# Top-32 attention feeding a two-layer MLP on one core: a hand-written drain, early copies on another engine, first attention products one slot later

## The chip, the cores and the metric

The kernel runs as one program on one core of a Trainium2 chip. The core has a matrix engine (TensorE, PE in the profile), a vector engine (VectorE, DVE), an activation engine (ScalarE, ACT), a general engine (GpSimd, POOL) and a queue processor that issues most transfers (SyncE, SP). Each engine takes its own instructions strictly in the order of its stream and waits on semaphores for the others. The metric is the device time of one execution in microseconds; the smaller the better. Times are medians of several executions.

## The reference, cut to what matters

```python
B, H, S, D = 8, 8, 576, 64
scores = q @ k.T / sqrt(D)                       # per batch and head, 576 x 576
kth    = 32nd largest of each row
attn   = softmax(where(scores >= kth, scores, -1e9))
x      = (attn @ v) -> [4608 tokens, 512]        # heads side by side
h      = x @ w_in                                # 512 x 2048
g      = max(h, 0) + alpha * min(h, 0)
out    = g @ w_out                               # 2048 x 512
```

So each of 64 x 576 rows of 576 scores needs its 32nd largest value, and everything below it is dropped before the softmax. The MLP follows on the tokens of a batch.

## The kernel before, in words

**Units.** A *duo* is two row blocks of 128 query rows by 576 scores: the same block j of the two heads of one pair p ("n" duos), or the last 64 rows of two pairs ("m" duos, the tails). The list `duos` (lines 77 to 83) has 18 duos for each of the 8 batches, 144 in all (ND). In a batch the order is blocks 0 and 1 of the four pairs, two tails, then blocks 2 and 3 of the four pairs; in the last batch the blocks go one after the other, block 0, tails, block 1, 2, 3.

**One slot per duo.** The main loop (line 722) runs slots n = 0 to ND + 3. Each engine's stream is written out by hand, since the wrapper `Ordered` (line 21) keeps program order; that wrapper issues every instruction, so every row of the profile names its line 32. A duo d goes through stages, each some slots later than the one before:

- slot d - 1: `st_qk` (233), scores in PSUM by TensorE; then `st_exit` (255), ScalarE copies them to SBUF (`s_sb`).
- slot d: `dve_slot` (313), VectorE takes the 8 largest of each of 6 groups of 96 columns (`up`, `small`) and, for each pair of duos, a lower bound of the 32nd largest (`p`, in `threshold_steps`, 285).
- slot d + 2: `st_count` (395), ScalarE counts by Sign which scores lie above the bound (`sg`); `st_y` (407), GpSimd multiplies the scores by the signs (`y`); then `row` (282), VectorE takes the 8 next candidates (`p` <- `y`).
- slot of the even partner + 4: the three `pick_steps` (265), VectorE picks the 32nd largest into KT, scaled by 2^60.
- slot d + 4: `st_relu` (414), ScalarE makes a bf16 tile that is huge wherever the score is below the 32nd largest (`r`), and GpSimd subtracts it from the scores in place (`s_sb` <- `s_sb`, `r`).
- slot d + 5: `st_exp` (422), ScalarE takes Exp of the masked scores into one of three tiles `w`, and SyncE issues the transpose of `w` into one of three tiles `wT`.
- slot d + 7: `st_av` (429), TensorE multiplies `wT` with v and a column of ones (an *AV*, 10 matmuls) into the single PSUM tile `xo`; at the odd duo of a pair `norm_a` and `norm_b` (454, 459) divide on VectorE, and `st_xT` (482) has the result of a whole block transposed by SyncE.

**The MLP beside it.** When a block's transposed tile is complete, `mlp_ready` (510) queues its work: *hidden units* `ph` (16 matmuls for 128 tokens, 512 values per partition), each followed by one Relu to `gT` on VectorE (`h_dve`, 566), and *output parts* `pz` (5 matmuls, four parts to 128 tokens), each four followed by one ScalarE copy `o_sb` (`o_act`, 577) and a store. The hidden units have two PSUM buffers, which the transposes of q and k and the filler matmuls (`rest`, `keep_warm`, 560) share; the output has one PSUM tile, so that parts wait for the copy. Blocks are taken as chunks of 256 tokens, in the last batch of 128 tokens. `h_pe` (547) and `o_pe` (572) place a unit or a part in a slot when there is one; otherwise the filler is placed.

**The start.** In slots 0 to 3 the transposed q and k (`tps`) are copied from PSUM to `qkT`; the copies of 512 columns (two each in slots 0 and 2) are on VectorE (line 773). The weights of the MLP are loaded and scaled in slots 2 to 15.

**The end.** Duos of the last four (140 to 143) have their own lags in `stage` (381 to 393); the four slots after 143 have the AVs first, and a loop (784) works off what is left of the MLP. Masking there goes as before: Relu on ScalarE, subtraction on GpSimd, Exp on ScalarE.

Of the kernel before, what the change touches and what calls it, by code (L numbers as in the profile page):

```python
# [8 lines left out]
FP32 = mybir.dt.float32  # L9
# [8 lines left out]
NG = 6  # L18
# [41 lines left out]
def fast_path(tc, q, k, v, moe_w_in, moe_w_out, moe_alpha, out, flag):  # L60
# [17 lines left out]
    for b in range(B):  # L78
        p0 = KPB * b
        last = b == B - 1  # L80
        half = lambda j, n: [("n", p, j + i) for p in range(p0, p0 + KPB) for i in range(n)]
        tails = [("m", p0, p0 + 1), ("m", p0 + 2, p0 + 3)]
        duos += half(0, 1) + tails + half(1, 1) + half(2, 1) + half(3, 1) if last else half(0, 2) + tails + half(2, 2)
# [4 lines left out]
    with ExitStack() as ctx:  # L88
# [171 lines left out]
        def norm_of(n):  # L260

            m = n - 7 if n < ND + 1 else {ND + 1: ND - 5, ND + 2: ND - 3, ND + 3: ND - 1}.get(n, 0)
            return m if m > 0 and m % 2 else 0
# [49 lines left out]
        def dve_slot(n, f_late):  # L313

            norm = norm_of(n)
            rows = [d for d in duos_at("row", n)]
            picks = [f for m in duos_at("pick", n) for f in pick_steps(m)]
            if on(n):
                s = T["s", n]
                if n % 2 == 0:  # L320
                    T["up", n // 2] = two.tile([128, 4, NG // 2, 8], FP32, name="up", tag="up")
                up = T["up", n // 2]
                for i in range(2):
                    r = 2 * (n % 2) + i
                    for g in range(NG):
                        o = 24 * r + 8 * (g // 2)
                        m = DVE.max(out=(lo if g % 2 else up)[:, r, g // 2, :],
                                    in_=s[:, i, GW * g:GW * g + GW])
                        if g % 2:
                            sm(m, [], [(o, o + 8)])  # L330
                            if picks:
                                picks.pop(0)()
                if n % 2 == 0:
                    h_dve()
                    for d in rows:
                        row(d, 0)
                    if norm:
                        norm_a(norm)
                    for d in rows:
                        row(d, 1)  # L340
                    if norm:
                        norm_b(norm)
                else:
                    fold, negate, least, turn = threshold_steps(n // 2)
                    fold()
                    h_dve()
                    negate()
                    for d in rows:
                        row(d, 0)
                    least()  # L350
                    turn()
                    for d in rows:
                        row(d, 1)
            else:
                if norm:
                    norm_a(norm)
                    norm_b(norm)
                early = picks and duos_at("pick", n)[0] < ND // 2 - 1
                if early:
                    for f in picks:  # L360
                        f()
                if not norm:
                    h_dve()
                for d in rows:
                    row(d, 0)
                    row(d, 1)
                if not early:
                    for f in picks:
                        f()
                if norm:  # L370
                    h_dve()
            if f_late:
                h_pe()
                h_dve()
# [6 lines left out]
        for d in range(ND):  # L381
            last = d - (ND - 4) if d >= ND - 4 else None
            for kind, lag, drain in (("count", 2, (2, 2, 2, 1)), ("relu", 4, (4, 3, 3, 2)),
                                     ("exp", 5, (5, 4, 4, 3)), ("av", 7, (6, 5, 5, 4))):
                at_slot = d + (lag if last is None else drain[last])
                if d < ND - 4:
                    at_slot = min(at_slot, ND + 1)
                stage.setdefault((kind, at_slot), []).append(d)
        for (kind, n), l in list(stage.items()):
            if kind == "count":  # L390
                stage["row", n] = l
        for m in range(ND // 2):
            stage["pick", 2 * m + (4 if m < ND // 2 - 1 else 3)] = [m]

        def st_count(n):
            s, p9 = T["s", n], T["p9", n // 2]
            sg = two.tile([128, 2, S], BF16, name="sg", tag="sg", bufs=3)
            if n % 2 == 0:
                T["cs", n // 2] = three.tile([128, 4], FP32, name="cs", tag="cs")
            cs = T["cs", n // 2]  # L400
            for i in range(2):
# [3 lines left out]
            T["sg", n] = sg  # L405
# [16 lines left out]
        def st_exp(n):  # L422
            w = ws[n % 3]
            ACT.activation(w[:, :, 0:S], T.pop(("s", n)), AF.Exp, scale=att_scale)
            wt = three.tile([128, 10, 128], BF16, name="wT", tag="wT")
# [3 lines left out]
        def st_av(n):  # L429
            d = duos[n]  # L430
            wt = T.pop(("wt", n))
            if n % 2 == 0:
                T["xo", n // 2] = ps_x.tile([128, 2, 2, 65], FP32, name="xo", tag="x")
# [48 lines left out]
        def st_xT(n):  # L482
            d = duos[n]
            b = d[1] // KPB
            if d[0] == "n":
# [3 lines left out]
                one = b == B - 1  # L489
# [18 lines left out]
        soon, hq, oq, act, stores, late_o = [], [], [], [], [], [0]  # L508
# [569 lines left out]
```

## Time and profile before

| | us |
|---|---|
| median of 3 executions | 839.28 (837.2 to 839.58) |
| the profiled execution's own time | 840.79 |
| its span, first to last instruction | 839.0 |

The profiled execution is 1.51 us above the median; 1.79 us of its own time lie outside its span. The page gives the busy time of each engine, the span in 40 slices, the chain of work that ended last, and groups of instructions with their mean duration and the idle time ahead of them. A row of the timeline reads: start, duration, engine, operation, output <- inputs, shapes, count, and in brackets the idle time before it with what ended it. Durations overlap by the pipeline's length, so what one more instruction costs in a row of equal ones is read from start to start.

### The profile page before, as it was taken

The page shows a single profiled execution, that of the slowest core. Times are in us where ns is not written, and L with a number is a line of the kernel's source. Part 1 is how long each engine was busy: PE and PEld are TensorE (multiplying, and loading weights), DVE is VectorE, ACT ScalarE, POOL GpSimd, SP SyncE. Part 2 cuts the span into 40 slices and gives each one's busy share as a digit, 9 for nine tenths or more (in the row PEclk, how much of TensorE's full clock was granted, in tenths as well). Part 3 has the DMA queues.
Part 4 walks back from the last instruction along what each step waited for, and adds up shares of the span by engine and source line. Part 5 has one row for each costly group of instructions (what it writes and reads, how often), then busy time and mean ns, then how long its engine had stood idle before and what let it go on. Part 6 is the DMA issues. An engine that isn't in the chain of part 4 may idle for free.

```text
span 839.0 us, 17803 instructions
## 1 busy us (share of the span) xinstructions
PE 751.4 (90%) x5382; PEld 426.0 (51%) x5382; DVE 759.2 (90%) x3475; ACT 763.5 (91%) x1255; POOL 753.7 (90%) x706
## 2 busy tenths in 40 slices
PE   8878798998989898898989899898989899989696
PEld 5334344555545554455545455555545555456463
DVE  4879977999999999999999999999999999999731
ACT  4789988999999999999999999999999999999820
POOL 1798988999999999999999999999999999999920
PEclk9979899999999999999999999999999999999898
DMA  6599867556656556556656556556666555444441
GB/s 142 157 165 182 157 124 151 92 122 134 118 120 131 109 103 148 107 133 120 128 114 142 112 96 143 107 132 121 131 113 142 120 96 103 88 83 79 81 87 41
DMA packets 344231, 100.19 MB, mean 119 GB/s; under 512 B 338032, under 2 KB 338048, under 8 KB 344128
## 3 DMA queue, kind: packets, MB, share of 16 engines
q1 hardware_dynamic: 341152, 92.13, 55.6%
q0 software_dynamic: 1776, 6.56, 3.2%
q8 instruction: 44, 0.72, 0.3%
q14 instruction: 59, 0.48, 0.2%
q10 hardware_dynamic: 1200, 0.30, 0.2%
HBM read 36.71 MB, written 9.44 MB: 55 GB/s over the span
## 4 chain that ended last, share of the span: by engine, by line
DVE 38%; POOL 19%; ACT 17%; PE 15%; issue 6%; DMA 3%; SPq 0%; ACTq 0%; POOLq 0%
DVE small L32 11%; DVE p L32 10%; POOL y L32 9%; POOL s_sb L32 9%; DVE up L32 7%; DVE gT L32 5%; ACT r L32 5%; ACT sg L32 5%; PE ps_sc L32 4%; ACT s_sb L32 4%; PE pz L32 3%; ACT w L32 3%; PE ph L32 3%; PE rest L32 2%; DMA wT<-w 2%
## 5 line engine op out<-in xcount | busy, mean ns | idle before, releaser
L32 POOL TENSOR_TENSOR y<-s_sb,sg 128x576 f32<-128x576 f32 x288 | 362.1, 1278 | 40.6 <-ACT sg L32 40.0
L32 POOL TENSOR_TENSOR s_sb<-s_sb,r 128x576 f32<-128x576 f32 x288 | 362.3, 1279 | 8.9 <-ACT r L32 8.6
L32 ACT ACTIVATE sg<-s_sb,p 128x576 bf16<-128x576 f32 x288 | 221.4, 773 | 8.0 <-DVE p L32 6.8
L32 DVE MAX8 p<-y 128x8 f32<-128x576 f32 x288 | 215.1, 747 | 8.1 <-POOL y L32 7.6
L32 DVE MAX8 up<-s_sb 128x8 f32<-128x96 f32 x864 | 211.8, 245 | 9.8 <-ACT s_sb L32 9.8
L32 DVE MAX8 small<-s_sb 128x8 f32<-128x96 f32 x864 | 216.1, 250 | 0.0
L32 ACT ACTIVATE r<-s_sb,KZ 128x576 bf16<-128x576 f32 x288 | 206.6, 769 | 0.4 <-DVE KZ L32 0.4
L32 PE MATMUL ps_sc<-qkT 64*128 64x512 f32 (+2 forms) x768 | 184.1, 569 | 18.7 <-ACT s_sb L32 18.6
L32 ACT COPY s_sb<-ps_sc 128x1152 f32<-128x1152 f32 x144 | 159.2, 1105 | 21.8 <-PE ps_sc L32 21.5
L32 ACT ACTIVATE w<-s_sb 128x1152 bf16<-128x1152 f32 x144 | 166.4, 1156 | 5.9 <-POOL s_sb L32 5.8
L32 PE MATMUL ph<-xT,w_in_b 128*128 128x256 bf16 (+1 forms) x1408 | 150.8, 255 | 5.3 <-ACT qkT L32 2.9
L32 PE MATMUL pz<-w_out_b,gT 128*128 128x512 bf16 x576 | 148.8, 381 | 0.3 <-DVE gT L32 0.3
L32 PEld LDWEIGHTS <-w_in_b 128*128 128x128 bf16 x1408 | 119.2, 99 | 48.7 <-issue 12.0
L32 PE MATMUL xo<-v,wT 128*128 128x65 bf16 (+3 forms) x1600 | 127.0, 199 | 11.2 <-DMA wT<-w 11.2
L32 PEld LDWEIGHTS <-wT 128*128 128x128 bf16 (+3 forms) x1600 | 97.9, 100 | 40.3 <-DMA wT<-w 11.8
L32 DVE TENSOR_SCALAR gT<-ph 128x512 bf16<-128x512 f32 x144 | 97.2, 675 | 19.4 <-PE ph L32 19.3
L32 PEld LDWEIGHTS <-gT 128*128 128x128 bf16 x576 | 55.9, 98 | 71.9 <-issue 16.9
L32 PEld LDWEIGHTS ps_sc<-qkT 64*128 64x128 f32 (+1 forms) x768 | 56.0, 170 | 64.4 <-ACT s_sb L32 30.3
L32 PEld LDWEIGHTS ps_sc<-kd,qkT 128*128 128x128 f32 x256 | 38.3, 189 | 97.7 <-issue 95.4
L32 PE MATMUL pz<-w_lin_b,xT 128*128 128x512 bf16 x144 | 55.6, 386 | 16.4 <-ACT o_sb L32 16.3
L32 PE MATMUL rest<-idle 128*128 128x512 bf16 x224 | 62.4, 409 | 8.6 <-DVE gT L32 5.2
L32 PE MATMUL ps_sc<-kd,qkT 128*128 128x128 f32 x256 | 62.8, 327 | 0.0
(57 smaller groups left out, 572.2 us busy)
## 6 DMA issues: line engine op xcount, KB each, us to landing
k_st<-in_k_dram SPq DMA_DIRECT2D x64, 128.0 KB, 2.8
v_st<-in_v_dram SPq DMA_DIRECT2D x64, 128.0 KB, 2.7
q_st<-in_q_dram SPq DMA_DIRECT2D x62, 128.0 KB, 2.8
out_dram<-o_sb SPq DMA_DIRECT2D x31, 256.0 KB, 2.5
w_st<-in_moe_w_out_dram POOLq DMA_DIRECT2D x4, 1024.0 KB, 6.6
wT<-w SPq DMA_TRANSPOSE x144, 3.5
w_in_b<-in_moe_w_in_dram POOLq DMA_DIRECT2D x4, 512.0 KB, 6.5
k_st<-in_k_dram SPq DMA_DIRECT2D x32, 32.0 KB, 2.7
```

Of the source, the lines that this page charges most:

```text
L32: ins = self.tc.keep_in_program_order(f(*a, **kw))
```

## The change

Four things are edited.

1. **The copies of the start.** The 512-column copies of `tps` to `qkT` in slots up to 3 are ScalarE's (`n > 3 and ...` in the condition).
2. **The first AVs.** For duos 0 to 12 the AV, and for the odd ones among them the normalization, come in slot d + 8 in place of d + 7; duos 12 and 13 fall together in slot 20.
3. **The next to last batch.** It ends with block 2 of the four pairs and then block 3, as two chunks of 128 tokens, in place of both blocks of each pair as one chunk of 256; the loads and transposes of pair 30 come two slots later.
4. **The drain.** The loop ends at slot 143. Behind it stands a list written out by hand. For duos 140 to 143 Relu and subtraction are gone: `st_all` takes Exp of the raw scores into an fp32 tile `e_sb`, and `st_mask` multiplies it on VectorE by (score >= 32nd largest), one instruction per row block, into `w`. The PSUM tile of the scores, free by then, becomes `spare`: its first bank is a second output tile, its two others hold the AVs of duos 140 to 143. Relus of hidden units go to VectorE and ScalarE by turns.

```diff
+        elif b == B - 2:
+            duos += half(0, 2) + tails + half(2, 1) + half(3, 1)
...
-            for kind, lag, drain in (("count", 2, (2, 2, 2, 1)), ("relu", 4, (4, 3, 3, 2)),
-                                     ("exp", 5, (5, 4, 4, 3)), ("av", 7, (6, 5, 5, 4))):
...
+            for kind, lag in (("count", 2), ("relu", 4), ("exp", 5), ("av", 8 if d < 13 else 7)):
+                stage.setdefault((kind, d + lag), []).append(d)
...
+            stage["norm", d + (8 if d < 13 else 7)] = d
...
-                one = b == B - 1
+                one = b == B - 1 or b == B - 2 and j > 1
...
-                on_dve = short and n > 16 or wide and (n < 17 or n % 2 == 0)
+                on_dve = n > 3 and (short and n > 16 or wide and (n < 17 or n % 2 == 0))
...
+        def picked(m):
+            for f in pick_steps(m):
+                f()
+            kv = T["kv", m] = two.tile([128, 4], FP32, name="kv", tag="kv")
+            DVE.tensor_scalar(kv, KT[:, 4 * m:4 * m + 4], 1.0 / BIG, None, ALU.mult)
+
+        def st_all(d):
+            e = T["e", d] = qk_p.tile([128, 2, S], FP32, name="e_sb", tag="qkT")
+            ACT.activation(e, T["s", d], AF.Exp, scale=att_scale)
+
+        def st_mask(d):
+            w, e, s_ = ws[d % 3], T.pop(("e", d)), T.pop(("s", d))
+            kv = T["kv", d // 2]
+            for i in range(2):
+                r = 2 * (d % 2) + i
+                DVE.scalar_tensor_tensor(out=w[:, i, 0:S], in0=s_[:, i, :], scalar=kv[:, r:r + 1],
+                                         in1=e[:, i, :], op0=ALU.is_ge, op1=ALU.mult)
+            st_wT(d)
...
+        def fill(k):
+            for _ in range(k):
+                if not o_pe() and not h_pe(2):
+                    keep_warm()
+
+        D = ND - 1
+        now[0] = ND
+        T["spare"] = ps_s.tile([128, 1536], FP32, name="spare", tag="s")
+        o_sp()
+        st_av(D - 6)
+        h_pe(2)
+        h_pe(2)
+        st_count(D - 1)
+        st_y(D - 1)
+        picked(D // 2 - 1)
+        h_relu()
+        normed(D - 6)
+        h_relu()
+        o_act()
+        st_all(D - 3)
+        st_all(D - 2)
+        fill(1)
+        h_pe(2)
+        st_av(D - 5)
+        st_mask(D - 3)
+        st_mask(D - 2)
+        st_count(D, (0,))
+        h_relu(ACT)
+        st_count(D, (1,))
+        st_y(D)
+        fill(1)
+        h_pe(2)
+        st_exp(D - 4)
+        h_relu(ACT)
+        o_act()
+        now[0] += 1
+        for d in (D - 1, D):
+            row(d, 0)
+            row(d, 1)
+        st_all(D - 1)
+        st_all(D)
+        picked(D // 2)
+        st_mask(D - 1)
+        st_mask(D)
+        o_sp()
+        st_av(D - 3)
+        fill(2)
+        o_act()
+        st_av(D - 4)
+        fill(1)
+        st_av(D - 2)
+        fill(2)
+        o_act()
+        normed(D - 4)
+        normed(D - 2)
+        o_sp()
+        now[0] += 2
+        st_av(D - 1)
+        fill(1)
+        h_relu(ACT)
+        st_av(D)
+        normed(D)
+        o_act()
...
+        while hq or act or soon or oq or stores:
...
+            h_relu((DVE, ACT)[turn % 2])
```

`normed(d)` is `norm_a(d)`, `norm_b(d)` and the two `st_xT`; `h_relu` is `h_dve` with a choice of engine. Stores of the first five steps after slot 143 are issued by GpSimd, before only in three slots.

More of the change, by code (lines that the diff above doesn't have):

```diff
@@ L315, in dve_slot @@
             norm = norm_of(n)
-            rows = [d for d in duos_at("row", n)]
+            rows = duos_at("count", n)
             picks = [f for m in duos_at("pick", n) for f in pick_steps(m)]
[L318 to L353, printed above, removed]
-            else:
[L355 to L371, printed above, removed]
@@ new lines, in dve_slot @@
+            s = T["s", n]
+            if n % 2 == 0:
+                T["up", n // 2] = two.tile([128, 4, NG // 2, 8], FP32, name="up", tag="up")
+            up = T["up", n // 2]
+            for i in range(2):
+                r = 2 * (n % 2) + i
+                for g in range(NG):
+                    o = 24 * r + 8 * (g // 2)
+                    m = DVE.max(out=(lo if g % 2 else up)[:, r, g // 2, :],
+                                in_=s[:, i, GW * g:GW * g + GW])
+                    if g % 2:
+                        sm(m, [], [(o, o + 8)])
+                        if picks:
+                            picks.pop(0)()
@@ L720, in fast_path @@
         PE.transpose(aps, a16, ident_f[0:NFT, 0:NFT])
-        for n in range(ND + 4):
-            end = n >= ND
+        for n in range(ND):
             now[0] = n
@@ L726, in fast_path @@
             o_sp()
-            if end:
-                for m in duos_at("av", n):
-                    st_av(m)
-            if not h_pe() and not end:
+            if not h_pe():
                 keep_warm()
@@ L749, in fast_path @@
                 st_exp(m)
[L750 to L751 removed]
+            if ready() > 4 or not wide_copy:
                 o_act()
```

128 lines of the change are left out of this document (78 added, 50 removed).

## The prediction

> **What bounds the kernel now.** I read the page's head first, then busy time by stretch (start and length, then each engine's busy us with its count, TensorE's granted clock, DMA share, GB/s).
>
> ```profile
> span 839.0 us, 17803 instructions
> 21.00:50.00 29.00, 21.91 (x94) 9.34 (x94) 25.25 (x106) 23.12 (x43) 23.82 (x26) 0.93 0.61 150
> 50.00:100.00 50.00, 41.35 (x234) 19.08 (x230) 43.91 (x195) 46.12 (x77) 45.71 (x46) 0.87 0.93 171
> 500.00:600.00 100.00, 91.54 (x656) 52.51 (x653) 98.98 (x463) 99.55 (x165) 99.56 (x91) 1.00 0.60 125
> 787.00:804.00 17.00, 9.80 (x91) 6.80 (x89) 7.33 (x15) 11.86 (x18) 14.17 (x13) 0.70 0.41 74
> 804.00:832.00 28.00, 26.30 (x257) 16.94 (x254) 9.29 (x16) 2.35 (x5) 0.00 (x0) 1.00 0.29 63
> ```
>
> Columns two to six are PE, weight loads, DVE, ACT, POOL. In the middle POOL, ACT and DVE are all at 99 of 100 us: they share the bound, and nothing in the change makes a middle slot shorter. The two ends have holes. From 21 to 50 us POOL works 23.82 of 29. From 787 to 804 TensorE works 9.8 of 17, and from 804 to 832 it is full alone: the end is its backlog. So the question is how much earlier each hole closes.
>
> **The start (edits 1 and 2).** Rows of PE, DVE, ACT and POOL, in brackets the idle time ahead:
>
> ```profile
> 22.70 0.78 ACT L32 ACTIVATE sg<-s_sb,p 128x576 bf16<-128x576 f32 x1
> 24.19 1.27 DVE L32 COPY qkT<-tps 128x512 f32<-128x512 f32 x2
> 24.91 3.09 PE L32 MATMUL rest<-idle 128*128 128x512 bf16 x8 [2.39 <-DVE qkT L32]
> 29.95 1.12 ACT L32 COPY s_sb<-ps_sc 128x1152 f32<-128x1152 f32 x1 [5.62 <-PE ps_sc L32]
> 32.81 2.52 POOL L32 TENSOR_TENSOR y<-s_sb,sg 128x576 f32<-128x576 f32 x2 [5.11 <-ACT sg L32]
> 54.79 1.07 PE L32 MATMUL xo<-v,wT 128*128 128x65 bf16 x10 [3.05 <-DMA wT<-w]
> 62.17 1.12 ACT L32 COPY s_sb<-ps_sc 128x1152 f32<-128x1152 f32 x1 [3.22 <-PE ps_sc L32]
> 65.36 2.52 POOL L32 TENSOR_TENSOR y<-s_sb,sg 128x576 f32<-128x576 f32 x2 [2.48 <-ACT sg L32]
> ```
>
> This is one chain twice. In slot 2 VectorE copies `tps` only behind its rows; the filler waits for those PSUM buffers, the scores of duo 4 stand behind the filler, ScalarE idles 5.62 us and GpSimd 5.11. With the copies on ScalarE they stand ahead of the count at 22.7, are done at about 23.8, and push that count into the idle time; the scores follow about 3.5 us earlier. Next late is VectorE: its bound for duos 2 and 3 comes some 0.9 us earlier and the pick of KT a good 2.6 us earlier than now, and ScalarE's Relu waits for that pick. I take **-2.6**. It costs ScalarE four copies of some 0.5 us (a copy of that size, `o_sb`, takes 0.58 in a row below), hidden in that idle time and in the like of it in slot 0; without that cover it is +2.0.
>
> In slot 7 TensorE waits 3.05 us for the first `wT`, the scores of duo 9 stand behind it, ScalarE idles 3.22, GpSimd 2.48. An AV one slot later has some 5.5 us more. Behind it stand that slot's filler and transposes, which are early enough. I take **-3.2**, together **-5.8**. What the edit adds: slots up to 20 hold a normalization beside the threshold steps and slot 20 a second AV of 0.7 us. I cost these at nothing, hidden in the 8.65 us that TensorE is free between 50 and 100; without the cover +0.7. Bounds: GpSimd's holes, 5.11 + 2.48 = 7.6, are the most; -2 if the DMA queues (share 0.93 at 50 to 100) make the next wait.
>
> **The last slots (edit 3).** Counted in the issue order, 15 hidden units and 18 output parts stand behind the last score matmul where 16 and 20 stood: they move ahead of it, where fillers stood. They bring one Relu more to VectorE among the last dozen slots:
>
> ```profile
> L32 DVE TENSOR_SCALAR gT<-ph 128x512 bf16<-128x512 f32 x144 | 97.2, 675 | 19.4 <-PE ph L32 19.3
> 774.30 0.78 ACT L32 ACTIVATE sg<-s_sb,p 128x576 bf16<-128x576 f32 x1 [0.45 <-DVE p L32]
> ```
>
> ScalarE waits for VectorE there, so I charge it in full: **+0.6** (0.675 less overlap).
>
> **The drain (edit 4).** Pieces of the chain that ended last (start, length), then rows:
>
> ```profile
> 803.42 1.17 ACT w L32
> ...
> 804.61 3.76 DMA wT<-w
> ...
> 808.42 0.79 PE xo L32 x10
> ...
> 816.85 0.89 PE ph L32 x16
> 817.75 1.09 PE pz L32 x5
> ...
> 831.99 0.58 ACT o_sb L32
> ```
>
> ```profile
> 775.94 1.13 PE L32 MATMUL ps_sc<-qkT 64*128 64x512 f32 x4
> 777.32 0.78 PE L32 MATMUL xo<-v,wT 128*128 128x65 bf16 x10
> 786.49 0.78 PE L32 MATMUL xo<-v,wT 128*128 128x65 bf16 x10
> 792.40 1.07 PE L32 MATMUL xo<-v,wT 128*128 128x65 bf16 x10 [5.13 <-DMA wT<-w]
> 784.60 0.75 DVE L32 MAX8 p<-y 128x8 f32<-128x576 f32 x1
> 785.27 0.16 DVE L32 RECIPROCAL KZ<-xo 128x4 f32<-128x4 f32 x1
> 785.81 0.20 DVE L32 TENSOR_TENSOR small<-small,cs 128x36 f32<-128x36 f32 x1
> 786.04 0.20 DVE L32 SCALAR_TENSOR_TENSOR pk<-small,p 128x36 f32<-128x36 f32 x1
> 784.78 0.78 ACT L32 ACTIVATE sg<-s_sb,p 128x576 bf16<-128x576 f32 x1 [1.07 <-DVE p L32]
> 785.55 0.76 ACT L32 ACTIVATE sg<-s_sb,p 128x576 bf16<-128x576 f32 x1
> 787.83 1.15 ACT L32 ACTIVATE w<-s_sb 128x1152 bf16<-128x1152 f32 x1
> 788.88 2.76 ACT L32 ACTIVATE r<-s_sb,KZ 128x576 bf16<-128x576 f32 x4
> 785.73 4.98 POOL L32 TENSOR_TENSOR y<-s_sb,sg 128x576 f32<-128x576 f32 x4
> 798.40 4.98 POOL L32 TENSOR_TENSOR s_sb<-s_sb,r 128x576 f32<-128x576 f32 x4 [2.77 <-ACT r L32]
> ```
>
> From start to start: a count 0.77, an Exp 1.05, a GpSimd pass 1.24, a VectorE row 0.67, a step of the pick 0.23 (four of them now, 0.9), a normalization 0.54, a unit 0.90, a part 1.09, an AV 0.72; a transpose lands 3.7 after its issue. Eight GpSimd passes (9.9 us) and eight ScalarE Relus leave; four Exps and eight masks come. I follow the new order on the old clock, the start's shift left out.
>
> - ScalarE: counts of 142 from 784.8 to 786.3, `o_sb` to 786.8, Exp of 140 and 141 to 787.9 and 788.9, count of 143 with a Relu of about 0.5 between its rows to 791.0, Exp of 139 to 792.1, Relu, Exp of 142 and 143 to 794.7.
> - GpSimd: `y` of 142 to 788.2; of 143 at 791.0 and 792.3, later than now (790.7), since Exps stand ahead of the count.
> - VectorE: free at 785.3; pick, Relu, normalization, Relu (0.6 each) to 787.95; masks of 140 and 141 to 789.35 and 790.7; rows of 142 and 143 to 793.4; pick to 794.3. The mask of 142 writes the tile that the transpose of 139 still reads, until 792.1 + 3.7 = 795.8: this is the new late wait. Masks of 142 and 143 then end at 797.15 and 798.5; now the last `w` is done at 803.42 + 1.17 = 804.6.
> - TensorE: idle from 785.4 to 786.9 (a PSUM buffer), then work to 790.5, idle until `wT` of 140 at 793.1, then nearly full: AV 143 at 802.5 to 803.2. Behind it stand 8 units, 10 parts and a transpose of 0.2: 7.2 + 10.9 + 0.2 = 18.3, so 821.5, the last copy ends at 822.1 in place of 832.57. **-10.5**.
>
> Check by TensorE's sum: from 777.32 stand 9 AVs, 15 units, 18 parts: 6.5 + 13.5 + 19.6 = 39.6 us, so 816.9 without a hole; the holes above make up the rest. The second output tile removes the wait of parts for the copy.
>
> A mask is an operation that no row shows. The nearest rows are the VectorE row of 576 columns (0.67 a step) and GpSimd's product of two such tiles (1.24 a step). I take 0.67, the same engine and width; below it nothing speaks for a gain. At 1.24 the masks of 142 and 143 end 2.3 us later, and so does the end: +2.3.
>
> The clock: after 5.13 us of idling the AV row takes 1.07 in place of 0.78, and at the start eight fillers after 2.39 us of idling take 3.09, where other rows have 2.12:
>
> ```profile
> 18.06 2.12 PE L32 MATMUL rest<-idle 128*128 128x512 bf16 x8
> ```
>
> The new hole of 2.6 us is like the start's, so I charge the work of 793 to 797 by the clock of 0.70 and let the next wait take some: **+1.2**. [...]
>
> The mask of 141 (789.35 to 790.7) lies beside `y` of 143 (from 789.7), both reading SBUF. [...]
>
> **The sum**: -5.8 + 0.6 - 10.5 + 1.2 = **-14.5**. The profiled execution's own 840.79 becomes 826.3; it lies 1.51 above the median of 839.28, which becomes 824.8. I say 825.
>
> **Rivals.**
> - *The start's gain is taken back.* Slots 8 to 23 also load weights and form the products of the MLP's weights; POOL had only 4.3 us free in 50 to 100, with the DMA at 0.93. If all but 1 us is lost: 825 + 4.8 = 829.8. For it speaks the DMA share, against it that the holes end on TensorE's order and not on loads.
> - *The drain gains half.* The chain Exp 139, transpose, mask 142, transpose, AV 142 is stretched (masks at 1.24, the transposes of five tiles in one queue): +5, so 830.
> - *Slower: the AV one slot later holds up SyncE.* `wT` has three tiles, so the transpose of duo d + 3, issued in slot d + 8, must wait for AV d in that same slot, and loads of q and k stand behind it in SyncE's queue. By the order, AV d ends about 2.1 us after the slot's first copy (scores 1.38 and the AV 0.72), the Exp of d + 3 after 2.6 (two counts, an Exp): a margin of 0.5. If TensorE is later than that, each of 13 slots pays; from 1.1 us a slot the gain is gone, at 1.3 the time is 825 + 13 x 1.3 = 842. Against it: between Exp and AV lie three slots, 15 us, for a transfer of 3.7.
> - *The edits do nothing in the start and the drain's order waits elsewhere* (both first rivals): 834.6.
>
> **How the numbers follow.** Forecast 0.64 (own range 822 to 828), start lost 0.15, half the drain 0.13, slower 0.05, both 0.03. The most is -7.6 for the start and no clock loss: 822; a Relu and waits that I charged but are hidden give 2 us more. The range 820 to 832 holds all but the last two. A measurement here can tell about 0.3% (2.5 us) from no change: faster 0.93, within 0.02 (from the case of both lost), slower 0.05.
>
> **What would show it.** Right: GpSimd's second `y` pair near 29.4 with its hole down to some 2 us; no wait for `wT` near 55; slots at 500 to 600 as before; the last `w` some 6 us earlier against the last score matmul; a VectorE wait ahead of the mask of 142; TensorE full for the last 18 us. Wrong: masks above 1 us, POOL holes growing between 60 and 160, SyncE waiting for `xo` in slots 8 to 20, or TensorE idle behind AV 143.

## The result, and the profile after

| | before | changed |
|---|---|---|
| median, us | 839.43 (837.2 to 839.79) | 824.96 (823.83 to 836.72) |
| the profiled execution's own time | 840.79 | 825.79 |
| its span | 839.0 | 823.8 |
| ratio of the times | | 0.9829, 95% interval 0.9802 to 0.9855 |

Four executions each; the ratio leaves out the one of 836.72, and the median of the other three is 824.14. The forecast was 825, from 840.79 to 826.3 for the profiled execution. So the total is right to half a microsecond. Its terms are not: the start brought 2.8 us more than predicted and the drain some 3 us less. That the two errors cancel is luck.

The time by stretch of the changed kernel (start, length, busy us of PE, weight loads, DVE, ACT and POOL, granted clock, DMA share, GB/s); the last two stretches are those of before moved by 9 us, since the last score matmul comes 8.6 us earlier. (Here and below that is the start of the last row of four 512-column score matmuls, 775.94 before and 767.38 now.)

```profile
21.00:50.00 29.00, 23.39 (x116) 10.30 (x115) 26.39 (x119) 27.01 (x50) 26.46 (x29) 1.00 0.71 179
50.00:100.00 50.00, 41.38 (x237) 19.14 (x235) 47.98 (x213) 49.56 (x83) 48.49 (x48) 0.93 0.97 179
500.00:600.00 100.00, 91.42 (x658) 52.75 (x657) 99.19 (x463) 99.64 (x165) 99.55 (x90) 1.00 0.61 125
778.00:795.00 17.00, 12.75 (x94) 7.28 (x94) 14.65 (x25) 9.23 (x15) 7.05 (x7) 0.80 0.52 107
795.00:823.00 28.00, 22.25 (x236) 15.23 (x234) 5.43 (x11) 4.74 (x8) 0.00 (x0) 0.99 0.21 55
```

From 21 to 50 POOL does 26.46 us where it did 23.82, from 50 to 100 48.49 where it did 45.71: together 5.4 of the 8.6 us. The middle is what it was. In the drain GpSimd is out of the bound, yet TensorE still stands still for 4 of 17 us, and the mean clock there is 0.80.

Where the time goes is seen best by laying the two traces beside each other. This table gives the start of ScalarE's copy of the scores of a duo, changed minus before, in us:

| duo | 0 | 3 | 4 | 8 | 9 | 16 | 17 | 18 | 22 | 63 | 122 | last score matmul | last output part |
|---|---|---|---|---|---|---|---|---|---|---|---|---|---|
| shift | +0.4 | +0.6 | -2.6 | -2.6 | -5.9 | -6.0 | -7.2 | -8.7 | -8.7 | -8.6 | -8.5 | -8.6 | -14.7 |

There are three steps in the start: at duo 4, at duo 9, and one that the prediction had not named, at duos 17 and 18. A hundred slots then add nothing. (Between duos 123 and 143, where edit 3 moves work about, the copies are up to 2 us less early, -6.6 at duo 138 and -8.1 at 143; the last score matmul is not.) The drain, from the last score matmul to the last output part, takes 48.85 us (816.23 - 767.38) in place of 54.94 (830.88 - 775.94): -6.1.

The rows of the start, on ACT, PE and POOL:

```profile
23.33 1.08 ACT L32 COPY qkT<-tps 128x512 f32<-128x512 f32 x2
23.97 1.89 PE L32 MATMUL rest<-idle 128*128 128x512 bf16 x8 [0.82 <-ACT qkT L32]
27.37 1.12 ACT L32 COPY s_sb<-ps_sc 128x1152 f32<-128x1152 f32 x1 [1.45 <-PE ps_sc L32]
30.21 2.51 POOL L32 TENSOR_TENSOR y<-s_sb,sg 128x576 f32<-128x576 f32 x2 [1.90 <-ACT sg L32]
53.92 0.79 PE L32 MATMUL xo<-v,wT 128*128 128x65 bf16 x10
56.29 1.10 ACT L32 COPY s_sb<-ps_sc 128x1152 f32<-128x1152 f32 x1
99.70 1.62 PE L32 MATMUL xo<-v,wT 128*64 128x65 bf16 x20
```

The filler starts at 23.97 in place of 24.91; its eight matmuls take 1.89 us at a granted clock of 1.00, where the 3.09 us of before went with 0.59. The copy of duo 4 waits 1.45 us in place of 5.62, and GpSimd 1.90 in place of 5.11. The first AVs wait for nothing. The last row is the AV of a tail: it waits for nothing either, and in the kernel before it did, by this row that the prediction did not have:

```profile
102.75 1.77 PE L32 MATMUL xo<-v,wT 128*64 128x65 bf16 x20 [2.55 <-DMA wT<-w]
109.78 1.12 ACT L32 COPY s_sb<-ps_sc 128x1152 f32<-128x1152 f32 x1 [1.01 <-PE ps_sc L32]
116.22 1.12 ACT L32 COPY s_sb<-ps_sc 128x1152 f32<-128x1152 f32 x1 [1.41 <-PE ps_sc L32]
```

ScalarE's two waits behind it, 1.01 and 1.41, make up 2.4 of the 2.7 us of the third step. It is the same chain as that of 54.79, 48 us later: an AV that waits 2.55 us for its transposed tile, and scores queued behind it.

The drain of the changed kernel, by engine (DVE, POOL, ACT, SyncE's transposes as SPq, PE):

```profile
777.85 1.08 DVE L32 TENSOR_SCALAR kv<-KZ 128x4 f32<-128x4 f32 x1
780.59 5.04 DVE L32 SCALAR_TENSOR_TENSOR w<-s_sb,kv,e_sb 128x576 bf16<-128x576 f32 x4
788.87 0.17 DVE L32 TENSOR_SCALAR kv<-KZ 128x4 f32<-128x4 f32 x1
790.80 3.00 DVE L32 SCALAR_TENSOR_TENSOR w<-s_sb,kv,e_sb 128x576 bf16<-128x576 f32 x4 [1.76 <-DMA wT<-w]
777.64 2.52 POOL L32 TENSOR_TENSOR y<-s_sb,sg 128x576 f32<-128x576 f32 x2
781.74 3.28 POOL L32 TENSOR_TENSOR y<-s_sb,sg 128x576 f32<-128x576 f32 x2 [1.58 <-ACT sg L32]
782.80 1.15 ACT L32 ACTIVATE w<-s_sb 128x1152 bf16<-128x1152 f32 x1
785.70 1.37 SPq L32 DMA_TRANSPOSE wT<-w  x1
787.18 1.47 SPq L32 DMA_TRANSPOSE wT<-w  x1
779.58 1.05 PE L32 MATMUL ph<-xT,w_in_b 128*128 128x128 bf16 x16 [2.06 <-DVE gT L32]
790.72 0.79 PE L32 MATMUL xo<-v,wT 128*128 128x65 bf16 x10 [2.08 <-DMA wT<-w]
791.45 0.60 PE L32 MATMUL pz<-w_lin_b,xT 128*128 128x512 bf16 x1
791.84 1.91 PE L32 MATMUL pz<-w_out_b,gT 128*128 128x512 bf16 x4
798.32 0.78 PE L32 MATMUL spare<-v,wT 128*128 128x65 bf16 x10
816.23 1.03 PE L32 MATMUL pz<-w_out_b,gT 128*128 128x512 bf16 x4
```

Read it from the top. Four mask steps take 5.04 us where GpSimd works beside them and 3.00 where it does not, and the tile `kv` takes 1.08 us in place of 0.17 in the same way. Not all of the four are slow:

```profile
L32 DVE SCALAR_TENSOR_TENSOR w<-s_sb,kv,e_sb x8: 809/812/1835, 780.6 to 793.0; 128x576 bf16<-128x576 f32 x8
```

That is the shortest, the median and the longest of the eight steps, in ns. The two of duo 140 start at 780.59 and 781.32 and take 0.81 us each. GpSimd's `y` of 143 begins at 781.74; the two steps of 141, from 782.04 and 783.80, run beside it and take 1.83 us each, and `y` itself takes 3.28 in place of 2.52. So the mask of 141 ends at 785.63 and its transpose is issued at 785.70. Exp of 139 is done at 783.95, but its transpose stands behind that of 141 in SyncE's stream, is issued at 787.18, and AV 139 starts at 790.72 after 2.08 us without work on TensorE. The clock is low for a while behind it: granted 0.50 from 791.84 to 793.75, 1.91 us for four matmuls that took 1.03 at 787.62, where it was 1.00. From AV 143 at 798.32 TensorE is full to 817.26. The late `kv` has a price too: the Relu behind it starts only at 778.85, and that is what TensorE's hole of 2.06 us ahead of 779.58 waits for.

### The profile page after: what moved, and what is told of

It is laid out like the page before. It is cut to its first block, busy times and chain, and to the rows that moved or that the text cites. A ratio compares the mean times of both kernels' runs of the same rounds, so it can differ in the third digit from the quotient of the medians.

```text
span 823.8 us, 17880 instructions
## 1 busy us (share of the span) xinstructions
PE 742.5 (90%) x5422; PEld 424.1 (51%) x5422; DVE 760.5 (92%) x3474; ACT 763.4 (93%) x1258; POOL 745.4 (90%) x700
## 3 DMA queue, kind: packets, MB, share of 16 engines
q0 software_dynamic: 1872, 6.82, 3.5%
## 4 chain that ended last, share of the span: by engine, by line
DVE 40%; ACT 19%; PE 19%; POOL 12%; issue 6%; DMA 2%; SPq 1%; ACTq 0%; POOLq 0%
DVE small L32 12%; DVE p L32 10%; DVE up L32 7%; POOL y L32 6%; ACT r L32 5%; POOL s_sb L32 5%; ACT sg L32 5%; PE ps_sc L32 5%; DVE gT L32 5%; ACT s_sb L32 4%; PE pz L32 4%; PE ph L32 4%; ACT w L32 3%; PE xo L32 2%; DVE qkT L32 2%
## 5 line engine op out<-in xcount | busy, mean ns | idle before, releaser
L32 POOL TENSOR_TENSOR s_sb<-s_sb,r 128x576 f32<-128x576 f32 x280 | 352.1, 1278 | 6.1 <-ACT r L32 5.8
L32 PE MATMUL ps_sc<-qkT 64*128 64x512 f32 (+2 forms) x768 | 182.1, 563 | 23.2 <-ACT s_sb L32 23.1
L32 ACT ACTIVATE r<-s_sb,KZ 128x576 bf16<-128x576 f32 x280 | 201.0, 768 | 0.3 <-DVE KZ L32 0.3
L32 ACT ACTIVATE w<-s_sb 128x1152 bf16<-128x1152 f32 x140 | 161.7, 1155 | 1.2 <-POOL s_sb L32 1.0
L32 PE MATMUL pz<-w_out_b,gT 128*128 128x512 bf16 x544 | 140.6, 381 | 0.4 <-DVE gT L32 0.4
L32 PE MATMUL xo<-v,wT 128*128 128x65 bf16 (+1 forms) x1560 | 123.4, 198 | 2.4 <-DMA wT<-w 2.1
L32 DVE TENSOR_SCALAR gT<-ph 128x512 bf16<-128x512 f32 x137 | 92.5, 675 | 10.0 <-PE ph L32 10.0
L32 PE MATMUL pz<-w_lin_b,xT 128*128 128x512 bf16 x136 | 52.7, 388 | 15.7 <-ACT o_sb L32 15.5
L32 PE MATMUL rest<-idle 128*128 128x512 bf16 x200 | 53.2, 394 | 7.4 <-DVE gT L32 5.4
```

The lines of the kernel that those rows point to most:

```text
L32: ins = self.tc.keep_in_program_order(f(*a, **kw))
```

## The experiments

Theory T1: the mask of 141 and GpSimd's `y` of 143 hold each other up, that makes the transpose of 141 late, and the order in SyncE's queue makes that of 139 late with it. T2: the wait of the mask of 142 for its tile (1.76 us in the row above), which the prediction had as the new late wait. T3: the low clock alone. For the start, theory A holds that edits 1 and 2 bring all three steps, the record that they bring 5.8. Times are medians; the kernel before had 839.3, 840.5 and 839.8 in the three groups of runs. Beside the median stands what one profile shows: the shift of the scores, and the length of the drain from the last score matmul to the last output part (54.94 before, 48.85 changed). Four profiles of the old drain give 54.94, 55.59, 55.36 and 55.44, three of the new one 48.85, 48.92 and 48.19: that is how far such a length can be trusted, 0.7.

**Edits 1 and 2 alone** (the kernel before with both).

```diff
-                on_dve = short and n > 16 or wide and (n < 17 or n % 2 == 0)
+                on_dve = n > 3 and (short and n > 16 or wide and (n < 17 or n % 2 == 0))
...
-                at_slot = d + (lag if last is None else drain[last])
+                at_slot = d + (lag if last is None else drain[last]) + (kind == "av" and d < 13)
...
```

Not shown: the normalization moves with its AV.

> The kernel before with edits 1 and 2 alone (ScalarE copies in slots up to 3; AVs and normalizations of duos 0 to 12 one slot later), its own drain kept. Theory of the traces: the score copies of slot 30 on come 8.6 us earlier and all of it reaches the end, about 830.8, because three waits go (the copies, the first wT, the wT of the tails). The record's price: 5.8 us, about 833.6, with the third wait counted as nothing.

Measured 833.9 us, ratio 0.9936 (0.9903 to 0.9969): by the median the record's number. In the profile all three steps are there, -9.25 from duo 3 to duo 23 (+2.36 to -6.89), but its first copy of scores comes 2.15 us late, and that is kept to the end. So the steps are A's and the median is the record's; in this profile the late first copy lies between, and whether the same holds for the other executions is not shown.

**Edit 1 alone** and **edit 2 alone**, each half of that diff.

> The kernel before with edit 1 alone. Theory of the traces: only the first hole closes, the copies from slot 4 on come about 2.6 to 3.2 us earlier, about 836.5. Rival, the middle's bound takes it back: copies after slot 30 as before, about 839.4.

Measured 837.32 us, ratio 0.9982 (0.9958 to 1.0007).

> The kernel before with edit 2 alone. Theory of the traces: two steps, 3.3 us at the copy of duo 9 and 2.7 at those of duos 17 and 18, about 833.5. The record's price: one step of 3.2, about 836.2. Slower rival (SyncE held up by AVs): above 840.

Measured 835.06 us, ratio 0.9949 (0.9927 to 0.9971). The profiles tell more than the medians. First the rows of edit 1 alone, then those of edit 2 alone:

```profile
52.96 1.07 PE L32 MATMUL xo<-v,wT 128*128 128x65 bf16 x10 [4.70 <-DMA wT<-w]
100.79 1.62 PE L32 MATMUL xo<-v,wT 128*64 128x65 bf16 x20 [2.34 <-DMA wT<-w]
```

```profile
24.98 3.57 PE L32 MATMUL rest<-idle 128*128 128x512 bf16 x8 [2.39 <-DVE qkT L32]
56.67 0.79 PE L32 MATMUL xo<-v,wT 128*128 128x65 bf16 x10
102.44 1.62 PE L32 MATMUL xo<-v,wT 128*64 128x65 bf16 x20
```

With edit 1 alone the scores are 3.2 us earlier from duo 3 to duo 4 (+0.7 to -2.5), then the first AV waits 4.70 us in place of 3.05, and 0.7 of the gain is lost again (duo 8: -2.5, duo 9: -1.7); the wait at the tails stays. Edit 2 alone brings -3.3 at duo 9 and -2.7 at duos 17 and 18, -6.0 in all. So the third step is edit 2's, and edit 1 keeps all of its step only with edit 2 behind it. The medians cannot show this: edit 1 brings 2.0 alone, with some 2 us to either side, and 1.2 on top of edit 2 (835.06 to 833.9).

**Edits 3 and 4 alone** (the changed kernel without 1 and 2).

```diff
-            for kind, lag in (("count", 2), ("relu", 4), ("exp", 5), ("av", 8 if d < 13 else 7)):
+            for kind, lag in (("count", 2), ("relu", 4), ("exp", 5), ("av", 7)):
...
-            stage["norm", d + (8 if d < 13 else 7)] = d
+            stage["norm", d + 7] = d
...
-                on_dve = n > 3 and (short and n > 16 or wide and (n < 17 or n % 2 == 0))
+                on_dve = short and n > 16 or wide and (n < 17 or n % 2 == 0)
```

> The changed kernel with edits 1 and 2 undone: edits 3 and 4 alone. Theory of the traces: the end is worth what is left, 14.5 less 8.6, so about 833.5. The record's price: 0.6 - 10.5 + 1.2 = -8.7, about 830.7.

Measured 832.44 us, ratio 0.9925 (0.9902 to 0.9949), between the two. The drain is 48.92 us, as in the changed kernel, and the copies of the late slots lose 0.4 (-1.67 at duo 117, -1.27 at duo 143), but the last score matmul loses nothing (-1.72), so that this 0.4 lies inside the drain's length. The scores, though, are 1.6 us earlier by duo 4 (+0.35 to -1.28), where nothing was edited. TensorE's eight filler matmuls there take 1.89 us, as at the granted clock of 1.00 in the changed kernel's profile, in place of the 3.09 of the kernel before, where it was 0.59:

```profile
25.27 1.89 PE L32 MATMUL rest<-idle 128*128 128x512 bf16 x8 [2.39 <-DVE qkT L32]
```

The spans add up: -6.7 (832.3) for edits 1 and 2, -8.6 (830.4) for 3 and 4, together -15.3 where the changed kernel has -15.2. That is in part chance, since the first of these spans holds a start 2.15 us late and the second 1.6 us of clock. The medians give -5.4 and -6.9, together -12.3 where the changed kernel has -14.5; each has an interval of 2 to 3 us to either side, so they do not speak against a sum.

**Without edit 3** (its loads go back too).

```diff
-        elif b == B - 2:
-            duos += half(0, 2) + tails + half(2, 1) + half(3, 1)
...
-                one = b == B - 1 or b == B - 2 and j > 1
+                one = b == B - 1
```

> The changed kernel without edit 3: the next to last batch ends in one two-block chunk again. Question: what do the one-block chunks bring? With them the copies of the scores at duo 138 to 143 come 0.1 to 1.3 us later or earlier than in the kernel before (end edits alone), about 0.4 in the middle of that. Theory A (the prediction's bookkeeping taken further): one hidden unit and two output parts, 0.90 + 2 x 1.09 = 3.1 us of TensorE, stand behind the last score matmul again, and TensorE is full for the last 18 us, so the end comes 3.1 - 0.4 = 2.7 us later than 825.0: 827.7 us. Rival B: this work fills TensorE's holes of the drain (2.06 and 2.08 us), then the end moves by -0.4 only: 824.6.

Measured 829.87 us, ratio 0.9877 (0.9855 to 0.9898): 4.9 above the changed kernel, further than either answer. (By the ratios it is 4.0, since the kernel before was 1 us slower in this group; by the spans 4.3.) The drain is 50.35 us, 1.5 longer. The other 3 arise at duo 22, long before the edited batch:

```profile
115.54 1.89 PE L32 MATMUL plin<-w_la,w_inT 128*128 128x512 bf16 x8 [2.15 <-ACT w_lin_b L32]
127.75 0.82 PE L32 MATMUL xo<-v,wT 128*128 128x65 bf16 x10 [2.57 <-DMA wT<-w]
```

In the changed kernel's own profile the same place reads

```profile
114.54 2.52 PE L32 MATMUL plin<-w_la,w_inT 128*128 128x512 bf16 x8 [2.15 <-ACT w_lin_b L32]
```

and no AV waits; the granted clock over that row is 0.72. With a full clock there (1.89 us for the eight matmuls), duo 20 is 1.6 us earlier (shift -9.36 from a first copy of +1.37, against -8.72 from +0.41); then the second of the two AVs that edit 2 puts into slot 20 waits 2.57 us, and duo 22 is at -5.68 in place of -8.72. Its transpose is issued at 121.63, at 120.90 in the changed kernel. The DMA issues of these moments, this kernel's and then the changed one's, with the us to landing in the last column:

```profile
wT<-w SPq DMA_TRANSPOSE x1, 6.1
```

```profile
wT<-w SPq DMA_TRANSPOSE x1, 4.0
```

So 2.1 of the wait is a slower transfer; with what it shares the DMA engines was not tested. The boundary itself was tested last.

**A fourth tile `w` for duo 142**, so that its mask waits for no transpose.

```diff
-            w, e, s_ = ws[d % 3], T.pop(("e", d)), T.pop(("s", d))
+            w, e, s_ = ws[3 if d == ND - 2 else d % 3], T.pop(("e", d)), T.pop(("s", d))
...
```

> The changed kernel with a fourth tile for the weights w, used by the mask of duo 142 alone, so that this mask does not wait for the transpose of 139 (VectorE waits 1.76 us there now). Theory T1 (the late transpose of 141, with that of 139 behind it in SyncE's stream, sets the end; the mask's wait is a consequence beside the path): the masks of 142 and 143 end 1.8 us earlier, but AV 139 stands ahead of their AVs and comes as late as now: 0 to -0.3, 824.8 us. Theory T2 (the wait of the mask of 142 is the new late wait, as the prediction had it): -1.8, 823.2 us.

Measured 824.80 us, ratio 0.9834 (0.9799 to 0.9869): the median of T1. The drain is 47.66 us, 1.2 shorter than 48.85, though only 0.5 shorter than the shortest of the three of its kind. AV 139 comes where it came (23.4 us behind the last score matmul, 23.3 in the changed kernel), as T1 has it, so the gain lies behind it:

```profile
790.14 0.79 PE L32 MATMUL xo<-v,wT 128*128 128x65 bf16 x10 [1.47 <-DMA wT<-w]
791.10 1.03 PE L32 MATMUL pz<-w_out_b,gT 128*128 128x512 bf16 x4
796.52 0.78 PE L32 MATMUL spare<-v,wT 128*128 128x65 bf16 x10
```

Behind a hole of 1.47 us in place of 2.08 the clock is full (1.03 in place of 1.91), and from AV 139 to AV 143 it is 6.4 us (796.52 - 790.14) in place of 7.6 (798.32 - 790.72). In the changed kernel AV 142 (796.70) waits for no tile, so T2's wait was not what counted there, and T3 is worth 1.2. Whether the fourth tile has a part in the shorter hole, one profile of each cannot tell.

**`y` of 143 on VectorE**, so that GpSimd is idle beside the masks.

```diff
-        st_y(D)
+        for i in range(2):
+            DVE.tensor_tensor(yl[:, i, :], T["s", D][:, i, :], sgl[:, i, :], ALU.mult)
...
```

> The changed kernel with the products y of duo 143 on VectorE in place of GpSimd, so that no GpSimd pass lies beside the masks of 140 and 141. Theory T1 (mask and GpSimd pass lock each other out; the late mask of 141 makes its transpose late and with it that of 139): the two steps of the mask of 141 take 0.75 to 0.8 each in place of 1.83, the transposes of 141 and 139 are issued 2 us earlier, AV 139 comes about 2 us earlier and the hole of 2.08 us ahead of it goes; with less of the slow clock the end comes 2 to 3.3 us earlier: 822.3 us. T2 (the wait of the mask of 142): the same transpose moves, -2.4 at the most: 822.6 us. T3 (the low clock alone sets the drain's length, whatever the masks do): 0, 825.0 us. A rival to all: two more VectorE instructions of about 0.75 us make the pick of 142 and 143 later, and the masks of 142 and 143 with it: +0.5, 825.5 us.

Measured 823.84 us, ratio 0.9805 (0.9783 to 0.9826). The tile's view, then PE:

```profile
L32 DVE SCALAR_TENSOR_TENSOR w<-s_sb,kv,e_sb x8: 809/812/818, 781.9 to 792.4; 128x576 bf16<-128x576 f32 x8
```

```profile
790.13 0.79 PE L32 MATMUL xo<-v,wT 128*128 128x65 bf16 x10
796.19 0.79 PE L32 MATMUL spare<-v,wT 128*128 128x65 bf16 x10 [1.39 <-DMA wT<-w]
```

No step is above 0.82 us: the 1.83 came from GpSimd's pass. The last score matmul is at 768.66 here, so AV 139 comes 21.5 us behind it in place of 23.3, without a hole. The drain is 47.06, 1.8 shorter. The next wait is AV 142's, 1.39 us.

**The transpose of 141 behind that of 139 in SyncE's stream**; masks and GpSimd stay as they are.

```diff
-        st_mask(D - 2)
+        st_mask(D - 2, False)
...
         st_exp(D - 4)
+        st_wT(D - 2)
...
```

> The changed kernel with the transpose of duo 141 issued behind that of 139 in SyncE's stream instead of ahead of it; masks and GpSimd passes stay as they are, so the masks still take 1.83 us each. Exp of 139 ends at 783.95 in the changed kernel, the mask of 141 at 785.6. T1 by its last part (the order in SyncE's stream makes AV 139 late): the transpose of 139 is issued at 784 in place of about 787.2, AV 139 comes 2 us or more earlier, that of 141 comes some 2 us later than now, but its AV stands behind that of 139 anyway; the end comes 2 to 2.7 us earlier: 822.6 us. Rival (the two transposes together are late, whatever their order): 0, 825.0 us. T3 (clock alone): 0.

Measured 824.55 us, ratio 0.9838 (0.9794 to 0.9883).

```profile
783.94 1.35 SPq L32 DMA_TRANSPOSE wT<-w  x1
780.55 5.04 DVE L32 SCALAR_TENSOR_TENSOR w<-s_sb,kv,e_sb 128x576 bf16<-128x576 f32 x4
788.57 0.78 PE L32 MATMUL xo<-v,wT 128*128 128x65 bf16 x10
794.53 0.79 PE L32 MATMUL spare<-v,wT 128*128 128x65 bf16 x10 [1.14 <-DMA wT<-w]
```

The masks are as slow as ever, 5.04 us; the transpose of 139 is issued 3.2 us earlier, AV 139 starts at 788.57, the hole is gone, and the drain is 46.77 us, 2.1 shorter. So it was the order in the queue through which the late mask reached TensorE. Again the wait of AV 142, 1.14 us, keeps the rest; its tile is made when VectorE's rows and pick let the mask of 142 begin, at 789.09.

By their medians these three kernels differ little from the changed one (0.2 to 1.1 us). In the profiles the ground ahead of the drain scatters by more than that (duo 143 at -6.82 to -8.73). Hence a last group, with the boundary of edit 2 moved behind the loads of the MLP's weights:

```diff
-            for kind, lag in (("count", 2), ("relu", 4), ("exp", 5), ("av", 8 if d < 13 else 7)):
+            for kind, lag in (("count", 2), ("relu", 4), ("exp", 5), ("av", 8 if d < 17 else 7)):
...
-            stage["norm", d + (8 if d < 13 else 7)] = d
+            stage["norm", d + (8 if d < 17 else 7)] = d
```

> The changed kernel with the AVs of duos 0 to 16 one slot later in place of duos 0 to 12, so that the slot with two AVs is 24 in place of 20. Question: the profiles of two kernels that differ from the changed one only near the end show duo 20 earlier by 1.6 to 1.7 us (eight matmuls of plin in 1.89 us in place of 2.52, behind the same idle time of 2.15 us), and then a wait of 2.2 to 2.6 us for wT ahead of the second AV of slot 20, after which duo 22 is some 3 us later than in the changed kernel. Theory F (edit 2's boundary has a wait that shows whenever TensorE's clock isn't low there): with the boundary at 24, behind the loads of the MLP's weights, neither profile nor runs show that wait; the time is that of the changed kernel, 825.0, or 1.6 us less, 823.4, by the clock at plin. Rival: the second AV is waited for at 24 as well, or the longer lag makes another wait: 825 to 828 us.

Measured 826.21 us (824.18 to 827.4), ratio 0.9845 (0.9824 to 0.9866). In the profile the wait is gone with a full clock at `plin`:

```profile
114.57 1.89 PE L32 MATMUL plin<-w_la,w_inT 128*128 128x512 bf16 x8 [2.15 <-ACT w_lin_b L32]
123.44 0.78 PE L32 MATMUL xo<-v,wT 128*128 128x65 bf16 x10
```

Up to duo 19 it is the changed kernel's profile to 0.03 us, then duo 22 is at -10.33 where that had -8.72, and 0.7 is lost at duos 27 to 29, at the new boundary. The span is 822.1, 1.7 less; the median is 1.3 more, in the range of the rival. So theory F holds in the profiled execution, the fastest of the five. The others have a lower granted clock (0.986 to 0.988, against 0.992) and take 1.2 to 3.2 us more; what they do stays open.

**The same without edit 3**, **with the queue's new order**, and **with the fourth tile and `y` on VectorE**: the diffs are those above.

> The same as the kernel with the boundary at duo 17, without edit 3 as well. Without edit 3 and with the boundary at 13 the time was 829.9, 4.9 above the changed kernel; from the last score matmul to the end that run needs 50.35 us in place of 48.85, and its copies lose nothing near the end where the changed kernel loses 0.4: so edit 3 would bring 1.1, and the other 3 us or so would be the wait at slot 20. Theory F: 1.1 above the kernel with the boundary at 17 and edit 3: 824.5 to 826.1. Rival (edit 3 brings nearly 5 us by itself): 828.3 to 829.9.

Measured 828.20 us, ratio 0.9868 (0.9845 to 0.9891): 2.0 above the kernel with the boundary at 17. The drain is 51.17 us in place of 48.19. Taking both pairs, edit 3 shortens the drain by 1.5 to 3.0 us. The 0.4 that it costs at the copy of duo 143 is within that.

> The boundary at duo 17 and, in the drain, the transpose of 141 issued behind that of 139. The second alone shortened the stretch from the last score matmul to the last output part from 48.85 to 46.77 us in the profile, by 2.1. Theory T1 and F: 2.1 less than the kernel with the boundary at 17 alone: 821.3 to 822.9. Rival (profiles of single executions misled, as the medians 824.55 and 824.96 of the two kernels with the boundary at 13 would have it): 0.4 less: 823 to 824.6.

Measured 824.03 us (823.91 to 824.2), ratio 0.9816 (0.9797 to 0.9836): 2.2 less than with the boundary alone, the predicted difference, though both lie higher than expected. The drain is 46.74, the length that the profile with the other boundary had (46.77), and 1.5 less than the 48.19 with the boundary alone. The spans differ by only 0.3 (821.8 and 822.1), since this profile met a low clock at `plin` (3.44 us for the eight matmuls) and comes to the drain 1.2 us later. So the profiles show the shorter drain, but not that the 2.2 between the medians is owed to it.

> The boundary at duo 17 and, in the drain, y of duo 143 on VectorE and a fourth tile w for duo 142. y on VectorE alone shortened the stretch from the last score matmul to the last output part by 1.8 us and left a wait of 0.58 us ahead of the mask of 142, which the fourth tile takes away. Theory T1: both add up, 2.4 less than the kernel with the boundary at 17 alone: 821.0 to 822.6. Rival (what follows is bound by VectorE's rows and pick, or by TensorE): 1.8 less: 821.6 to 823.2.

Measured 824.07 us (823.66 to 831.29), ratio 0.9827 (0.9801 to 0.9853): 2.1 less, where 1.8 was the rival's and 2.4 T1's; the drain is 46.90, 1.3 less than with the boundary alone. The two repairs of the drain do not add up: AV 142 then waits 1.3 us for its tile.

Two of its six executions took 829.45 and 831.29 us, and the longer one is the profiled one. Its first copy is 1.4 us later than that of the changed kernel, and from duo 9 to duo 13 it loses 5.2 us (shift -4.07 to +1.14), though up to slot 19 this kernel does what the changed one does. Rows of PE and ACT, then the transposes issued between 50 and 75 us with the median us from issue to landing, here and in the changed kernel's profile:

```profile
71.06 1.06 PE L32 MATMUL xo<-v,wT 128*128 128x65 bf16 x10 [4.12 <-DMA wT<-w]
71.10 1.16 ACT L32 ACTIVATE w<-s_sb 128x1152 bf16<-128x1152 f32 x1 [3.62 <-DMA wT<-w]
wT<-w SPq DMA_TRANSPOSE x4, 13.2
```

```profile
wT<-w SPq DMA_TRANSPOSE x6, 6.9
```

So an AV can wait in the start even one slot later, and ScalarE with it, when the transposes land some 6 us later. Why they did so in this execution, and whether the longer executions of other kernels have the same, was not tested.

Five kernels have a lower median than the changed one (the lowest 823.84, against 824.96; against the 824.14 of its three other executions it is three kernels). Their intervals overlap with its interval: none is shown to beat it.

## Why the prediction was right in sum and wrong in its terms

- **Edit 1, -2.6: right in size, in part by luck.** The step is -3.2 from duo 3 to 4, but the profile of before had its filler at a low clock there (granted 0.59, 3.09 us for eight matmuls in place of 1.89). With the old copies and a full clock (edits 3 and 4 alone) duo 4 is 1.6 us earlier as well, so the edit is worth about 1.6 in an execution with a full clock, by an estimate from these two shifts. The prediction also added edits 1 and 2 as if they were independent: alone, edit 1 loses 0.7 again at the first AV.
- **Edit 2, -3.2: half of it.** The step at duo 9 is -3.3 as worked out. The failed step is that the prediction names one wait for `wT`, the first. Later AVs took away the wait of 2.55 us at 102.75 too, another -2.7, so that the start is -8.6 in place of -5.8, and beyond the most that was allowed, 7.6. On the other side "I cost these at nothing" failed at slot 20: its second AV waited 2.57 us in one profile and 2.20 in another, where the prediction had 0.7 us of TensorE and no wait. In the changed kernel's own profile that wait did not show.
- **Edit 3, +0.6: near** as a cost (0.4 at the copy of duo 143). With that included, the work that moved ahead of the last score matmul shortened the drain by 1.5 to 3.0. The prediction had the gain inside the drain's count: one unit and two parts, 3.1, so 2.5 with the cost.
- **Edit 4, -10.5 + 1.2: too much by 3.2** (-6.1). The failed step is "masks of 140 and 141 to 789.35 and 790.7". On the old clock (8.56 us later) they began at 789.15, 1.2 after the 787.95 of the forecast, most of it by `kv` (1.08 us, where a step of the pick was put at 0.23). The second ended at 794.2, 3.5 late: from start to start the steps took 0.73 and 1.76 us in place of 0.67. So the prediction's own sign of being wrong came, masks above 1 us, and the last `w` is 2.2 us earlier against the last score matmul, not 6. From there it goes on through a step that was not written at all: SyncE has the transpose of 139 behind that of 141, so it was issued at 795.7 in place of 792.1. AV 143 came at 806.9 in place of 802.5, 4.4 late, of which the term for the clock had covered 1.2.
- **What stands behind it was right**: a wait ahead of the mask of 142 (1.76 us), TensorE full behind AV 143, 18.2 us where 18.3 was summed.
- **The masks beside `y`.** The prediction set the mask of 141 beside `y` of 143 and put no term for it into the sum. The trace shows a cost: a mask step takes 1.83 us beside `y` and 0.81 without, and `y` itself 3.28 in place of 2.52. What comes late by it is the mask of 141, and SyncE's queue passes that on.
- **The clock.** The prediction charged its new hole of 2.6 us by the start's row, where the clock was low behind 2.39 us of idling (granted 0.59). In the drain it was low behind 2.08 us of idling (granted 0.50 over the four matmuls from 791.84). The term of 1.2 was right in size: 7.6 us in place of 6.4 from AV 139 to AV 143. It was charged for a hole of 2.6 us ahead of AV 140, though; that one is 0.60, and the hole behind which the clock was low stands ahead of AV 139.

The rivals: in the changed kernel's profile the start's gain was not taken back, and the view of SyncE's waits from 40 to 125 us names no wait for an AV, so the slower case did not come. In the profile of 831.29 us 5.2 us of the gain were lost, behind late transposes: the first rival can come in part in single executions. "The drain gains half" was nearest to the truth in the drain, by another mechanism.

## What to carry to other kernels

When a lag is changed because of one wait, list every wait of that kind in the stage that the lag reaches: here there were two, and the second was worth 2.7 us. When an operation moves to VectorE, look for GpSimd work beside it (here a mask step took 1.83 us in place of 0.81), and follow what it delays through the issue order of every queue behind it, not only along its own data. Add an aligned table of one repeated event (here a copy per slot) to any comparison of two traces: it shows at once in which slots a difference arises, and a sum that comes out right does not hide two errors.

## What the runs showed of the hardware

- **The clock differed between executions behind the same hole.** Eight matmuls behind 2.39 us of idling took 3.09 us (before, granted clock 0.59), 3.57 (edit 2 alone) and 1.89 (edits 3 and 4 alone); behind 2.15 us of idling 2.52 (changed, granted clock 0.72) and 1.89 (without edit 3). Kernels that do the same up to that row had it at different clocks; what decides it, no run shows. The first copy of scores began at 9.17 us (before), 9.58 (changed), 10.54 (without edit 3) and 11.32 (edits 1 and 2 alone). The six warm-up matmuls (`warm`) ahead of it took 0.88 us in the first two, 1.51 in the third and 1.54 in the last, and the 2.15 us by which the last is later than before are kept to the end.
- **Earlier was later.** With a full clock at `plin` duo 20 came 1.6 us earlier and duo 22 3 us later, because the AV then waited for its tile (2.57 us), whose transfer took 6.1 us in place of 4.0. It came a second time with `y` on VectorE (full clock, a wait of 2.20 us).
- **A GpSimd pass held up even a small VectorE instruction**: `kv`, 128 x 4 values from SBUF to SBUF, took 1.08 us beside a GpSimd pass and 0.17 without. Not each one: `p<-small` of the same size, which reads PSUM, took 0.17 at 776.43 beside a pair of GpSimd passes (775.04 to 777.56); what sets the two apart was not tested.
- **In the drain a transpose of `w` held SyncE's stream for 1.3 to 1.5 us** (rows above) and landed about 3.5 us after its issue (787.18 to 790.7); those of 141 and 139 were issued 1.5 us apart (785.70 and 787.18). Beside the loads of the start the median to landing was 6.9 us in one profile and 13.2 in another.
